# Reordering the work around the turning of chunk 1's keys and queries in an attention + MLP kernel on one core

## The chip, the cores and the metric

The kernel runs on one core of a Trainium2 chip. The metric is the device time of one execution in microseconds (us). Before the change four executions took 233.51, 233.23, 233.58 and 234.99 us; their median is 233.55 us. One further execution was recorded by the hardware profiler. It took 234.79 us, and 233.0 us of that are the span from the first to the last instruction of the program.

## The reference

Attention over 4 batches, 8 heads, 768 positions, 64 elements per head, followed by a two-layer MLP over all 3072 tokens:

```python
scores = scale * np.matmul(q, k.transpose(0, 1, 3, 2))
stream_keep = causal & (is_sink | in_win)           # first 4 keys, or the last 64
mask = np.where(retr[0, :, 0, 0, None, None], full_mask, stream_mask)
scores = np.where(mask[None, :, :, :], scores, -1000000000.0)
a = np.exp(scores - max); a = a / (a.sum + 1e-09)
attn = np.matmul(a, v)
x = attn.transpose(0, 2, 1, 3).reshape(B * S, H * D)   # 3072 x 512
h = x @ w_in                                        # 512 x 2048
g = np.maximum(0.01 * h, h)
out = g @ w_out                                     # 2048 x 512
```

Heads 0, 2 and 6 see all earlier keys; the other five see the first 4 keys (the sinks) and a window of 64. All inputs and the output are float32 in memory; the kernel computes in bfloat16 with float32 sums.

## The kernel before, in words

The 3072 tokens are cut into 8 chunks of 384 (half a batch each; the order is batch 0 first half, batch 1 first half, batch 0 second half, batch 1 second half, and then the same for batches 2 and 3). A chunk goes through attention, then "product 1" (x times w_in, 16 column tiles of 128, each closed by a leaky ReLU on ScalarE), then "product 2" (g times w_out, closed by a copy on VectorE and a store). The order of all instructions is written out by hand: each engine executes its own instructions in program order, and a semaphore wait holds up everything behind it on that engine. So "moving" a step means moving all its instructions on TensorE, VectorE and ScalarE alike.

Tiles that TensorE writes are PSUM banks with four tags, two banks each: `ph`, `psS`, `po`, `py`. A third user of a tag waits until the first has been emptied.

The start of the program treats chunk 0 in three tiles of 128 queries (objects `F0`, `F1`, `F2`), because its data arrive piecewise. `Fj.x_t` turns the finished attention rows of tile j (4 transposes on TensorE into a `py` bank, one copy by VectorE, "v", or ScalarE, "a"). `in_tile(q4, j)` is product 1 for tile j and column quarter q4 of w_in: 16 matmuls of 128x128 (L576) into one `ph` bank and one ScalarE instruction (L579). `in_tile(0, *)` needs the first quarter of w_in, `in_tile(1, *)` the second.

For chunk 1, `turn_pair(1, p, ...)` turns the keys or queries of the head pair p: three transposes (L203), one for each of three 128-row tiles that come by DMA. Keys are emptied in two halves (L190 on VectorE, L194 on ScalarE: "vv" both by VectorE, "aa" both by ScalarE); queries in one copy (L188 on VectorE, L192 on ScalarE) into `qt`. `zero_small(1)` clears two tiles of batch 1 on VectorE (L171, L172); `ats[2:]` are three tiles whose middle parts have to be zero (L736); `m_win0` is a mask; `sink_keys(1)` gathers the four sink keys of each head (L262, L266), `sink_values(1)` their values (L128). `a1` is the list of attention slots of chunk 1: a slot of a retrieval head computes scores into a `psS` bank (L329), ScalarE takes their exponential (L334), and VectorE multiplies by a causal mask (L337, L339). The value products follow six slots later.

All loads that convert float32 to bfloat16 are issued by POOL in program order at the head of the kernel (L638 to L655): chunk 0's tiles, the first quarter of w_in, chunk 1's k (three issues at L113), chunk 1's q (three at L113), the second quarter of w_in (L135), chunk 1's v, the rest of the weights, and then k, q and v of chunk 2.

Of the kernel before, what the change touches and what calls it, by code (L numbers as in the profile page):

```python
# [21 lines left out]
def kernel(  # L22
# [12 lines left out]
    nc = tc.nc  # L35
    B, H, S, D = q.shape
# [22 lines left out]
    def bank(tag, shape, dtype):  # L59
        return ps.tile(shape, dtype, name=tag, tag=tag, bufs=BANKS[tag])  # L60

    def bf(name, *shape):
        return one.tile([128, *shape], BF16, name=name)
# [13 lines left out]
    m_one = bf("m_one", 64)  # L77
    m_win = bf("m_win", 6, 64)
    m_win0 = bf("m_win0", 6, 64)
    m_sink = bf("m_sink", H)  # L80
    shift = bf("shift", 2, 128)
    kt = [[bf(f"kt{i}_{hh}", 4, S) for hh in range(2)] for i in range(2)]
    va = [bf(f"va{i}", 6, H, D + 1) for i in range(B)]
    vb = [bf(f"vb{i}", 5, H, D + 1) for i in range(B)]
    vs = [bf(f"vs{i}", H, D + 1) for i in range(2)]
    ksink = [bf(f"ksink{i}", 4 * SK) for i in range(2)]
    ats = [bf(f"ats{i}", 3, 4, 64) for i in range(5)]
# [38 lines left out]
    def sink_values(b, eng):  # L126
        n = H - 1
        eng.tensor_tensor(  # L128
            vs[b % 2][0:32, 1:H, 0:D],
            vsf[b].rearrange("p (o d) -> p o d", o=1).to_broadcast([32, n, D]),  # L130
            m_sink[0:32, 1:H].rearrange("p (h o) -> p h o", o=1).to_broadcast([32, n, D]),
            op=ALU.mult)
# [37 lines left out]
    def zero_small(i, eng):  # L170
        eng.memset(ksink[i][:], 0.0)  # L171
        eng.memset(vs[i][:], 0.0)  # L172
# [12 lines left out]
    def move(eng, dst, src, hh=None):  # L185

        if eng == "v" and hh is None:
            nc.vector.tensor_copy(dst, src)  # L188
        elif eng == "v":
            nc.vector.tensor_scalar_mul(dst, src, half[:, hh : hh + 1])  # L190
        elif hh is None:
            nc.scalar.activation(out=dst, in_=src, func=ACTF.Copy)  # L192
        else:
            nc.scalar.activation(out=dst, in_=src, func=ACTF.Copy, scale=half[:, hh : hh + 1])  # L194

    def turn_pair(n, p, tags, engs, nms="kq"):
        b, c = ORDER[n]
        if n not in qx:
            qx[n] = rot.tile([128, 4, CH], BF16, name="qt", tag="qt", bufs=1)
        for nm, tag, eng in zip(nms, tags, engs):  # L200
            pt = bank(tag, [128, 4, 128], BF16)
            for g in range(3):
                nc.tensor.transpose(pt[:, g, :], raw[nm, n][:, g, 2 * p : 2 * p + 2, :], ident[:])  # L203
            if nm == "k":
                for hh in range(2):
                    move(eng[hh], kt[b % 2][hh][:, p, CH * c : CH * c + CH].rearrange("p (g t) -> p g t", g=3), pt[:, 0:3, :], hh)
            else:
                move(eng, qx[n][:, p, :].rearrange("p (g t) -> p g t", g=3), pt[:, 0:3, :])
# [38 lines left out]
    def into(slots, extra):  # L247
        r, extra = [], list(extra)
        for j, s in enumerate(slots):
            r.append(s)  # L250
            if 5 * j >= 2 * len(slots) and extra:
                r.append(extra.pop(0))
                if len(extra) > len(slots) - j - 2:
                    r.append(extra.pop(0))
        return r + extra
# [14 lines left out]
    def sink_keys(b):  # L270
        for f in sink_keys_by(b):
            f()
# [282 lines left out]
    py = {}  # L555

    def in_slots(n, tags=("ph",)):
        def tick(t):
            if n not in gs:
                gs[n] = rot.tile([128, NG, CH], BF16, name="g", tag="g", bufs=2)  # L560
            ph = bank(tags[t % len(tags)], [128, 512], FP32)
            for g in range(KG):
                nc.tensor.matmul(ph[:, 0:CH], lhsT=w_in_bf[:, g, 128 * t : 128 * t + 128],  # L563
                                 rhs=xts[n][:, g, :] if n else xts[0][:, :, g, :], start=(g == 0), stop=(g == KG - 1))
            nc.scalar.activation(out=gs[n][:, t, :], in_=ph[:, 0:CH], func=ACTF.Prelu, alpha=0.01)  # L565

        return [lambda t=t: tick(t) for t in range(NG)]

    def in_tile(q4, j, tag="ph"):
        if 0 not in gs:  # L570
            gs[0] = rot.tile([128, NG, CH], BF16, name="g", tag="g", bufs=2)
        ph = bank(tag, [128, 4, 128], FP32)
        for x in range(4):
            t = 4 * q4 + x
            for g in range(KG):
                nc.tensor.matmul(ph[:, x, :], lhsT=w_in_bf[:, g, 128 * t : 128 * t + 128],  # L576
                                 rhs=xts[0][:, j, g, :], start=(x == 0 and g == 0),
                                 stop=(g == KG - 1), skip_group_check=True)
        nc.scalar.activation(out=gs[0][:, 4 * q4 : 4 * q4 + 4, 128 * j : 128 * j + 128], in_=ph[:],  # L579
                             func=ACTF.Prelu, alpha=0.01)  # L580
# [29 lines left out]
    def run(*lists):  # L610
        for l in lists:
            for f in l:
                f()

    def tail(ms, a):

        return [a[0], ms[0], a[1], ms[1], a[2], ms[2], ms[3], *a[3:]]

    def both(s, e):
        return lambda: (s(), e and e())  # L620
# [66 lines left out]
    F0, F1, F2 = (First(j) for j in range(3))  # L687
# [43 lines left out]
    F2.finish(0)  # L731
    F2.av(1)
    F2.finish(1)
    zero_small(1, nc.vector)
    for a in ats[2:]:
        nc.vector.memset(a[:, :, 1:3, :], 0.0)  # L736
    F1.x_t("py", "a")
    in_tile(0, 0)
    turn_pair(1, 0, ("psS",), ("vv",), "k")
    turn_pair(1, 1, ("psS",), ("aa",), "k")  # L740
    in_tile(0, 1)
    F2.x_t("py", "v")
    turn_pair(1, 2, ("psS",), ("vv",), "k")
    turn_pair(1, 3, ("py",), ("aa",), "k")
    in_tile(0, 2)
    turn_pair(1, 0, ("psS",), "v", "q")
    turn_pair(1, 1, ("py",), "v", "q")
    turn_pair(1, 3, ("psS",), "v", "q")
    turn_pair(1, 2, ("py",), "v", "q")
    nc.vector.tensor_copy(m_win0[:, 2:], m_one.rearrange("p (o t) -> p o t", o=1).to_broadcast([128, 4, 64]))  # L750
    sink_keys(1)
    sink_values(1, nc.vector)
    nc.vector.tensor_copy(vs[1][0:32, :, D], m_sink[0:32, :])
    p0 = in_slots(0)
    a1 = Attention(1, po_tags=("po", "po", "po", "py"), xt_eng="v").slots([0, 2, 6, 1, 3, 4, 5, 7], lag=6)


    run(a1[0:3])
    in_tile(1, 0)
    run(a1[3:5])  # L760
    in_tile(1, 1)
    run(a1[5:6])
    in_tile(1, 2)
# [28 lines left out]
    for n in range(2, NCH):  # L792
        a, extra = [], ()
# [10 lines left out]
        if n + 1 < NCH:  # L804
            a = Attention(n + 1, xt_eng="v", xt_tag="py", cross=n > 2).slots(lag=2 if n > 2 else 3)
            a = into(a, extra) if n > 2 else a
        ms = merge(in_slots(n), outs)
        keep = []
        if n == 2:
            a = [both(s, e) for s, e in zip(a, [None] * 16 + extra + [None] * 3)]  # L810
            ms, a, keep = ms[:-6], a[:-6], tail(ms[-6:-2], a[-6:]) + ms[-2:]
# [42 lines left out]
```

## Time and profile before

| quantity | value |
|---|---|
| median of four executions | 233.55 us (233.23 to 234.99) |
| the profiled execution, its own time | 234.79 us |
| its span | 233.0 us |
| TensorE (PE) busy | 223.6 us, 96% of the span |
| VectorE (DVE) busy | 98.8 us, 42% |
| ScalarE (ACT) busy | 127.5 us, 55% |
| GpSimd (POOL) busy | 71.1 us, 31% |
| granted TensorE clock | 0.999 of full speed |

A row of the timeline begins with the start in us from the span's start and the length in us; then come the engine, the line of the kernel, the operation, and output<-inputs. `x16` says how many instructions were merged. What stands in brackets is how long the engine idled before the row, and what ended that. `PEld` is the weight load that precedes a matmul. A row of the DMA list tells from which queue a transfer was issued, how often, the size of one, and the time from issue to landing. In the chain of waits each row is a piece of the path that ended last.

### The profile page before, as it was taken

The numbers are of one execution on the slowest core, as the hardware profiler recorded it, in microseconds if no ns is written. First come the engines' busy times: TensorE is split into PE (matmuls) and PEld (weight loads), VectorE is DVE, ScalarE is ACT, GpSimd is POOL, SyncE is SP. The second block draws the span as 40 slices with busy tenths as digits, with TensorE's granted clock in tenths as the row PEclk, the third lists the DMA queues.
The fourth block names the chain that finished last, engine by engine and source line by source line (L and its number), as shares of the span: only waits on it lengthen the run. The fifth ranks groups of instructions, "written<-read, shape, count | busy, mean of one in ns | idle before, by whom it ended". The sixth has DMA issues, their size and how long they took to land.

```text
span 233.0 us, 5091 instructions
## 1 busy us (share of the span) xinstructions
PE 223.6 (96%) x2054; PEld 139.3 (60%) x2080; DVE 98.8 (42%) x282; ACT 127.5 (55%) x275; POOL 71.1 (31%) x87
## 2 busy tenths in 40 slices
PE   6888999999999999999999999999999999999995
PEld 4666876644665676665556655666556665555554
DVE  7895568014566358358324451155212341111122
ACT  5766765722774886655355544765556763434300
POOL 8968534217319219439104800000000000000000
PEclk9999999999999999999999999999999999999999
DMA  9999999999999999999999992920210220111112
GB/s 130 151 165 178 203 207 169 180 130 160 150 149 257 180 160 131 173 177 158 135 142 188 172 172 57 209 65 17 68 59 0 65 80 20 45 45 45 45 47 91
DMA packets 109480, 28.98 MB, mean 124 GB/s; under 512 B 101248, under 2 KB 105744, under 8 KB 109456
## 3 DMA queue, kind: packets, MB, share of 16 engines
q0 software_dynamic: 77088, 13.39, 76.8%
q1 hardware_dynamic: 31312, 15.00, 32.5%
q10 hardware_dynamic: 1056, 0.26, 0.5%
q8 instruction: 16, 0.26, 0.5%
q14 instruction: 8, 0.07, 0.1%
HBM read 27.30 MB, written 6.29 MB: 144 GB/s over the span
## 4 chain that ended last, share of the span: by engine, by line
PE 86%; POOL 5%; DMA 4%; issue 1%; DVE 1%; ACT 0%; POOLq 0%
PE py L589 31%; PE ph L563 31%; PE po L298 7%; PE psS L329 5%; DMA w_in_bf<-in_moe_w_in_dram 4%; PE psS L589 3%; PE psS L364 3%; PE psS L563 2%; PE psS L309 2%; PE ph L576 1%; POOL kb L113 1%; POOL va L118 1%; POOL qb L113 1%; POOL k L104 1%; POOL q L105 1%
## 5 line engine op out<-in xcount | busy, mean ns | idle before, releaser
L563 PE MATMUL ph<-xt,w_in_bf 128*128 128x384 bf16 x448 | 90.4, 326 | 0.1
L589 PE MATMUL py<-w_out_bf,g 128*128 128x512 bf16 (+1 forms) x327 | 85.7, 374 | 1.2
L565 ACT ACTIVATE g<-ph 128x384 bf16<-128x384 f32 x112 | 55.0, 491 | 56.8 <-PE ph L563 56.4
L563 PEld LDWEIGHTS <-w_in_bf 128*128 128x128 bf16 x480 | 44.0, 98 | 30.7
L589 PEld LDWEIGHTS <-g 128*128 128x128 bf16 x416 | 35.8, 98 | 25.9
L334 ACT ACTIVATE at<-psS 128x384 bf16<-128x384 f32 x78 | 37.0, 488 | 17.4 <-PE psS L329 16.9
L595 DVE COPY o<-py 128x512 f32<-128x512 f32 (+1 forms) x22 | 14.9, 678 | 52.1 <-PE py L589 51.8
L113 POOL DMA_DIRECT2D kb<-in_k_dram x21 | 18.7, 908 | 32.2 <-DMA kd<-kb 31.6
L329 PE MATMUL psS<-qd,kt 128*128 128x384 bf16 (+2 forms) x90 | 23.2, 294 | 0.0
L118 POOL DMA_DIRECT2D va<-in_v_dram x24 | 21.4, 916 | 5.0 <-DMA w_out_bf<-in_moe_w_out_dram 1.8
L113 POOL DMA_DIRECT2D qb<-in_q_dram x21 | 18.6, 916 | 5.7 <-DMA w_in_bf<-in_moe_w_in_dram 1.8
L298 PE MATMUL po<-va,at 128*128 128x65 bf16 x228 | 19.3, 193 | 0.0
L369 ACT ACTIVATE ats<-psS 128x384 bf16<-128x384 f32 x35 | 16.9, 490 | 3.2 <-PE psS L364 2.9
L298 PEld LDWEIGHTS <-at 128*128 128x128 bf16 x234 | 14.9, 98 | 5.2 <-issue 0.2
L373 DVE TENSOR_TENSOR ats<-ats,m_win 128x384 bf16<-128x384 bf16 x35 | 12.4, 357 | 12.0 <-ACT ats L369 11.2
L237 DVE COPY kt<-kd 64x512 bf16<-64x512 bf16 x36 | 14.9, 413 | 2.0 <-DMA kd<-kb 1.4
L397 DVE TENSOR_TENSOR xs<-po,linv 128x384 bf16<-128x384 f32 x27 | 15.0, 557 | 0.9
L329 PEld LDWEIGHTS <-kt 128*128 128x128 bf16 x99 | 9.4, 98 | 7.4 <-issue 0.6
L364 PEld LDWEIGHTS <-kt 128*128 128x128 bf16 x210 | 10.5, 98 | 5.1 <-issue 0.2
L339 DVE TENSOR_TENSOR at<-at,m_caus 128x128 bf16<-128x128 bf16 x21 | 4.7, 224 | 20.1 <-ACT at L334 19.9
L298 PEld LDWEIGHTS <-ats 128*128 128x128 bf16 x210 | 10.5, 97 | 4.0 <-DVE xs L397 0.4
L337 DVE TENSOR_TENSOR at<-at,m_caus 128x256 bf16<-128x256 bf16 x21 | 6.1, 291 | 14.7 <-ACT at L334 14.7
(145 smaller groups left out, 204.3 us busy)
## 6 DMA issues: line engine op xcount, KB each, us to landing
out_dram<-o SPq DMA_DIRECT2D x23, 256.0 KB, 2.3
va<-in_v_dram POOLq DMA_DIRECT2D x24, 128.0 KB, 7.7
kb<-in_k_dram POOLq DMA_DIRECT2D x21, 128.0 KB, 5.5
qb<-in_q_dram POOLq DMA_DIRECT2D x21, 128.0 KB, 6.7
w_in_bf<-in_moe_w_in_dram POOLq DMA_DIRECT2D x4, 512.0 KB, 9.6
w_out_bf<-in_moe_w_out_dram POOLq DMA_DIRECT2D x4, 512.0 KB, 13.3
vb<-va SPq DMA_DIRECT2D x8, 195.0 KB, 4.0
vb<-va SPq DMA_DIRECT2D x4, 130.0 KB, 3.2
```

The lines of the kernel that those rows point to most:

```text
L113: nc.gpsimd.dma_start(out=t[:, g], in_=nat[nm][b, c, :, :, g])
L118: nc.gpsimd.dma_start(out=va[b][:, 3 * c + g, :, 0:D], in_=nat["v"][b, c, :, :, g])
L237: nc.vector.tensor_copy(kt[b % 2][hh][r, :, o : o + 128], raw["kx", n][r, g])
L298: nc.tensor.matmul(o, lhsT=lhsT, rhs=rhs, start=first, stop=False, skip_group_check=True)
L329: nc.tensor.matmul(s[:, off : off + w], lhsT=kt[i][hh][:, p, 128 * kj : 128 * kj + 128], rhs=q_of(n, p, lo, CH), start=(j == 0), stop=(j = ...
L334: nc.scalar.activation(out=a[:, 0:off], in_=s[:, 0:off], func=ACTF.Exp, scale=SM)
L364: nc.tensor.matmul(s[:, 64 * m : 64 * m + 64], lhsT=kt[i][hh][:, p, k0 : k0 + 128], rhs=q_of(n, p, 64 * m, 64 * m + 64), start=(m == 0), s ...
L369: nc.scalar.activation(out=av_, in_=s[:, 0:CH].rearrange("p (j e f) -> p j e f", j=3, e=2), func=ACTF.Exp, scale=SM)
L397: nc.vector.tensor_tensor(xs[:], po[:, :, :, 0:D], linv.to_broadcast([128, 3, 2, D]), op=ALU.mult)
L563: nc.tensor.matmul(ph[:, 0:CH], lhsT=w_in_bf[:, g, 128 * t : 128 * t + 128], rhs=xts[n][:, g, :] if n else xts[0][:, :, g, :], start=(g == ...
L565: nc.scalar.activation(out=gs[n][:, t, :], in_=ph[:, 0:CH], func=ACTF.Prelu, alpha=0.01)
L589: nc.tensor.matmul(py[n][:, 0 : c1 - c0], lhsT=gs[n][:, ng, 128 * tt : 128 * tt + 128], rhs=w_out_bf[:, ng, c0:c1], start=(ng == 0), stop= ...
```

## The change

The set of steps stays the same; their order between the end of chunk 0's attention and the second quarter of product 1 changes. Four things differ.

- The third x (`F2.x_t`) and `in_tile(0, 1)` go in front of the first turning of chunk 1's keys.
- The four turnings of q directly follow those of k. They use the two `py` banks alone (before: `psS` and `py` in turns), and the second is emptied by ScalarE instead of VectorE. All four key pairs use `psS`; of the fourth pair one half is emptied by VectorE, where ScalarE did both.
- `zero_small(1)` stands between the turnings of k and those of q instead of ahead of them.
- The clearing of `ats[2:]` and the filling of `m_win0` follow the first three slots of `a1`; `sink_values(1)` and the column beside it follow the next two.

```diff
     F2.finish(1)
+    F1.x_t("py", "a")
+    in_tile(0, 0)
+    F2.x_t("py", "v")
+    in_tile(0, 1)
+    turn_pair(1, 0, ("psS",), ("vv",), "k")
+    turn_pair(1, 1, ("psS",), ("aa",), "k")
+    in_tile(0, 2)
+    turn_pair(1, 2, ("psS",), ("vv",), "k")
+    turn_pair(1, 3, ("psS",), ("va",), "k")
     zero_small(1, nc.vector)
+    turn_pair(1, 0, ("py",), "v", "q")
+    turn_pair(1, 1, ("py",), "a", "q")
+    turn_pair(1, 3, ("py",), "v", "q")
+    turn_pair(1, 2, ("py",), "v", "q")
+    sink_keys(1)
+    p0 = in_slots(0)
+    a1 = Attention(1, ...).slots([0, 2, 6, 1, 3, 4, 5, 7], lag=6)
+    run(a1[0:3])
     for a in ats[2:]:
         nc.vector.memset(a[:, :, 1:3, :], 0.0)
-    F1.x_t("py", "a")
-    in_tile(0, 0)
-    turn_pair(1, 0, ("psS",), ("vv",), "k")
-    turn_pair(1, 1, ("psS",), ("aa",), "k")
-    in_tile(0, 1)
-    F2.x_t("py", "v")
-    turn_pair(1, 2, ("psS",), ("vv",), "k")
-    turn_pair(1, 3, ("py",), ("aa",), "k")
-    in_tile(0, 2)
-    turn_pair(1, 0, ("psS",), "v", "q")
-    turn_pair(1, 1, ("py",), "v", "q")
-    turn_pair(1, 3, ("psS",), "v", "q")
-    turn_pair(1, 2, ("py",), "v", "q")
     nc.vector.tensor_copy(m_win0[:, 2:], ...)
-    sink_keys(1)
+    in_tile(1, 0)
+    run(a1[3:5])
     sink_values(1, nc.vector)
     nc.vector.tensor_copy(vs[1][0:32, :, D], m_sink[0:32, :])
-    p0 = in_slots(0)
-    a1 = Attention(1, ...).slots([0, 2, 6, 1, 3, 4, 5, 7], lag=6)
-    run(a1[0:3])
-    in_tile(1, 0)
-    run(a1[3:5])
     in_tile(1, 1)
     run(a1[5:6])
     in_tile(1, 2)
```

No DMA is added, removed or moved: the instructions of POOL and of the store queue (SP) are the same ones in the same order. From `in_tile(1, 0)` on TensorE's instructions are the same in the same order.

More of the change, by code (lines that the diff above doesn't have):

```diff
@@ L733 @@
     F2.finish(1)
-    zero_small(1, nc.vector)
-    for a in ats[2:]:
-        nc.vector.memset(a[:, :, 1:3, :], 0.0)
     F1.x_t("py", "a")
     in_tile(0, 0)
+    F2.x_t("py", "v")
+    in_tile(0, 1)
     turn_pair(1, 0, ("psS",), ("vv",), "k")
     turn_pair(1, 1, ("psS",), ("aa",), "k")
-    in_tile(0, 1)
-    F2.x_t("py", "v")
+    in_tile(0, 2)
     turn_pair(1, 2, ("psS",), ("vv",), "k")
-    turn_pair(1, 3, ("py",), ("aa",), "k")
-    in_tile(0, 2)
-    turn_pair(1, 0, ("psS",), "v", "q")
-    turn_pair(1, 1, ("py",), "v", "q")
-    turn_pair(1, 3, ("psS",), "v", "q")
+    turn_pair(1, 3, ("psS",), ("va",), "k")
+    zero_small(1, nc.vector)
+    turn_pair(1, 0, ("py",), "v", "q")
+    turn_pair(1, 1, ("py",), "a", "q")
+    turn_pair(1, 3, ("py",), "v", "q")
     turn_pair(1, 2, ("py",), "v", "q")
-    nc.vector.tensor_copy(m_win0[:, 2:], m_one.rearrange("p (o t) -> p o t", o=1).to_broadcast([128, 4, 64]))
     sink_keys(1)
-    sink_values(1, nc.vector)
-    nc.vector.tensor_copy(vs[1][0:32, :, D], m_sink[0:32, :])
     p0 = in_slots(0)
@@ L758 @@
     run(a1[0:3])
+    for a in ats[2:]:
+        nc.vector.memset(a[:, :, 1:3, :], 0.0)
+    nc.vector.tensor_copy(m_win0[:, 2:], m_one.rearrange("p (o t) -> p o t", o=1).to_broadcast([128, 4, 64]))
     in_tile(1, 0)
     run(a1[3:5])
+    sink_values(1, nc.vector)
+    nc.vector.tensor_copy(vs[1][0:32, :, D], m_sink[0:32, :])
     in_tile(1, 1)
```

## The prediction

> **What bounds the kernel now.** I read the busy shares first (PE 96%), then the chain of waits around the changed place, then the timeline of PE, DVE and ACT there. The chain:
>
> ```profile
> 13.50 10.40 DMA w_in_bf<-in_moe_w_in_dram
> 23.90 0.05 issue
> 23.95 1.07 PE ph L576 x16
> ```
>
> The end hangs on a transfer: the second quarter of w_in, issued at 13.50, lands at 23.90, and in_tile(1,0) starts at 23.95. Behind it PE runs nearly without a hole. By busy time in windows, PE has 6.00 of 6.00 us in 24 to 30 and again in 30 to 36, and 11.95 of 12.00 in 36 to 48. Comparing starts, I find in 24 to 55 three small holes: 0.06 at 28.97 (two av rows end, the next starts at 29.03), 0.16 at 32.91, 0.22 at 36.24, together 0.44 us.
>
> The changed work lies in front of 23.95:
>
> ```profile
> 15.64 1.07 PE L576 MATMUL ph<-xt,w_in_bf 128*128 128x128 bf16 x16 [0.20 <-DVE linv L542]
> 17.90 0.44 PE L203 MATMUL psS<-ident,kb 128*128 128x128 bf16 x2 [1.20 <-DMA kb<-in_k_dram]
> 18.84 0.40 PE L203 MATMUL psS<-ident,kb 128*128 128x128 bf16 x4 [0.50 <-DMA kb<-in_k_dram]
> 19.07 1.06 PE L576 MATMUL ph<-xt,w_in_bf 128*128 128x128 bf16 x16
> 19.97 0.39 PE L550 MATMUL py<-ident,xs 128*128 128x128 bf16 x4
> ...
> 20.87 1.05 PE L576 MATMUL ph<-xt,w_in_bf 128*128 128x128 bf16 x16
> 21.76 0.33 PE L203 MATMUL psS<-ident,qb 128*128 128x128 bf16 x3
> ...
> 22.54 0.32 PE L329 MATMUL psS<-qt,kt 128*128 128x384 bf16 x1
> 23.07 0.70 PE L329 MATMUL psS<-qt,kt 128*128 128x256 bf16 x3 [0.20 <-DVE qt L188]
> ```
>
> The reader sees k's tiles awaited twice (1.20 and 0.50 us), then work without a hole up to the first score at 22.54. The third score starts at 23.44 (a narrower window gives this start) and streams 0.16, so PE would be free at 23.60. The weight load of in_tile(1,0) waits 0.67 us for the transfer:
>
> ```profile
> 23.95 0.90 PEld L576 LDWEIGHTS <-w_in_bf 128*128 128x128 bf16 x16 [0.67 <-DMA w_in_bf<-in_moe_w_in_dram]
> ```
>
> That is 0.35 us of slack (23.95 less 23.60). Making the front shorter can only enlarge it.
>
> **The change, part by part.**
>
> *Third x and in_tile(0,1) into the wait for k.* Sixteen matmuls from 19.07 to 19.97, 0.90 us, and four transposes, 0.22 (4 x 0.055), in all 1.12 us. in_tile(0,0) ends at 16.53 (15.64 + 0.89); F2's xs are ready at 16.05 (15.63 + 0.42 on DVE); so x_t runs 16.53 to 16.75 and in_tile(0,1) to 17.64, before k's first tile at 17.90. The filling works: 1.12 us leave the stretch behind 19.07. By itself this is a gain of 1.12 us in front of 23.95, and 0 behind it, because the transfer covers it. Without that cover it would be worth what the next wait leaves of it, computed now.
>
> *q straight behind k.* k pairs 0 and 1 turn at 18.84 to 19.07 as before; in_tile(0,2) then runs 19.07 to 19.96; pair 2 to 20.13. Pair 3 needs the bank that ACT empties by 20.33 (19.75 + 0.57 = 20.32) and turns at 20.4. Issues of q start at 10.91, 11.77 and 12.64 and land 8.8, 8.8 and 8.7 us later (the DMA list in narrow windows), so the third tile is there at 21.34. q's turning can thus start at most 0.42 us earlier than at 21.76. But its emptying has something in front of it. DVE, in the old order:
>
> ```profile
> 16.06 0.28 DVE L171 MEMSET ksink<- 128x272 uint32 x1
> 16.40 0.49 DVE L172 MEMSET vs<- 128x520 bf16 x1
> 16.88 0.63 DVE L736 MEMSET ats<- 128x192 uint32 x3
> 19.11 0.74 DVE L190 TENSOR_SCALAR kt<-psS,half 128x384 bf16<-128x384 bf16 x2 [1.60 <-PE psS L203]
> ...
> 20.75 0.74 DVE L190 TENSOR_SCALAR kt<-psS,half 128x384 bf16<-128x384 bf16 x2
> 22.13 0.36 DVE L188 COPY qt<-psS 128x384 bf16<-128x384 bf16 x1 [0.64 <-PE psS L203]
> 22.40 0.35 DVE L188 COPY qt<-py 128x384 bf16<-128x384 bf16 x1
> ```
>
> The two memsets lay under the wait for k, free. Now they lie behind k and ahead of q. From transposes to the first emptying took 0.37 (20.38 to 20.75), so pair 2 starts on DVE at 20.34. Three L190 (two of pair 2, one of pair 3, 0.33 apart and 0.41 long) end at 21.41; the memsets take 0.34 to the next start and 0.49, end 22.24. q's pair 0 is then emptied 22.24 to 22.60 (before from 22.13). Pair 3 needs its `py` bank, pair 2 follows: PE starts at 22.65 (0.05 from DVE's end to PE, as 22.49 to 22.54) and takes two times three transposes, 0.33. First score 22.98, against 22.54. ACT's exponential followed the score by 0.36 (22.54 to 22.90), and the third score that by 0.54 (22.90 to 23.44, the bank): 22.98 + 0.36 + 0.54 = 23.88, plus 0.16 of streaming, 24.04. in_tile(1,0) starts at 24.04 against 23.95: **+0.09 us**. What is late next is a1's exponentials, by 0.44; the fifth score needs the third's bank, emptied at about 24.7, and PE reaches it at 25.1.
>
> *One emptying of q on ACT, one half of k on DVE.* ACT loses one L194 (0.57) and gets a copy of 128x384 that the trace does not show on it. From below L334's 0.48, from above the 0.60 of L579; I take 0.57, L194's, the same shape from the same type. It starts at 21.8 and ends by 22.4, before PE needs the bank at 22.8. At either end it costs 0; if it had no cover, 0.2.
>
> *Fills behind the scores.* Three memsets (0.22 each) and the mask (0.21) come after the third mask on DVE, at about 24.9 to 25.7; the next L337 ran at 26.06. The zeros are used by value products from 31.78, m_win0 by L373 at 29.01. sink_values (0.61) and the column (0.17) follow L339 at 26.45 and end by 27.4; the L337 behind them ran at 27.32 and its result is used after 28.9. All 0, hidden by those waits; without that cover at most 0.1.
>
> *Queues.* POOL and SP keep their instructions. POOL's issues that wait for PE are chunk 2's k (25.50, after k is turned, by 20.8) and q (29.50, after q is turned, 23.0). Both have over 4 us: 0.
>
> *The sum.* +0.09 from the late scores, 0 from the rest. Bounds: if the weight quarter lands earlier in unprofiled executions, the two fronts are compared bare, 24.04 less 23.60, +0.44. From below, -0.05 (the step from landing to start) and -0.44 if all holes behind closed, -0.49. I take +0.1: the nearest row is the transfer's. The profiled execution would go from 234.79 to 234.9; that one is 1.24 us above the median. On the median: **233.65 us**.
>
> [...] PE does only transposes from 19.96 to 22.98, 3.0 us. In the old trace that stretch was 16.53 to 19.07, 2.5 us, and the granted clock was 1.00 in 16.71 to 20.12 (PE busy 1.72 of 3.41 us). [...]
>
> **The rivals.** A change of 0.5% is 1.17 us, about what a measurement here tells from none.
>
> *The front decides in every execution* (the quarter lands earlier without the profiler): +0.44, 234.0. For it: the median lies 1.24 us below the profiled time, and something was faster there. Against: k and q come through the same queue, and would come earlier too.
>
> *The clock falls* in the emptier stretch before 23.95. Price: the twenty dummy matmuls at the start.
>
> ```profile
> 1.06 3.66 PE L151 MATMUL psS<-blank 128*128 128x256 bf16 x20 [1.06 <-DVE blank L632]
> 27.14 0.60 PE L309 MATMUL psS<-qt,ksink 128*128 128x256 bf16 x4
> ```
>
> Cold, 19 steps of a 256-wide matmul took 3.39 us (3.66 less the last one's 0.27), 0.178 each; later 0.11 each ((0.60 - 0.27)/3). One such stretch behind 23.95 costs 19 x 0.068 = 1.3 us: 234.95, **slower**. It decides once the transposes-only stretch is longer than what the old trace survived (2.5 us); I expect 3.0. Against it: the transposes, twelve of q and six of k, are spread over the stretch, as the six of k were in the old one.
>
> *The filled wait is worth its length.* in_tile(1,0) at 22.83 and the holes closed: 233.55 - 1.12 - 0.44 = 232.0, **faster**. For it: 1.7 us of waits for k. Against it: the 10.40 us transfer, issued before anything that changes, and the memsets.
>
> *The change doesn't do what it says*, q being emptied no earlier, is part of my forecast.
>
> **How the numbers follow.** Forecast 0.70, front decides 0.12 (both within 0.5%), clock 0.11, full worth 0.07. Faster 0.07, same 0.82, slower 0.11. The range holds the first two with their bounds, -0.49 and +0.44 on 233.55, widened at either end by the 0.35 by which the three closest of the four runs differ: 232.7 to 234.4.
>
> **What would show it.** In the new profile: x_t and in_tile(0,1) between 16.5 and 17.7; DVE's memsets at 21.4 to 22.3 with the first q copy behind them; the first score near 23.0 and the third near 23.9; the quarter landing at 23.9 and in_tile(1,0) within 0.2 us of 24.0; PE full behind. I am wrong if the quarter lands at another time, if the clock is below 1.00 behind 24, or if a new hole opens between 24 and 36.

## The result, and the profile after

Over 54 executions the changed kernel has a median of 234.88 us (233.35 to 238.55). Over 78 executions of the kernel before, the first four among them, it is 233.88 us (232.91 to 236.97). The ratio is 1.0028 with a 95% interval of 1.0015 to 1.0040: slower, by less than 0.5%. Ratios, here and below, leave out executions over 1.5% above the fastest of their kernel (eight of the 54, two of the 78); the medians leave out none, and differ by 1.0 us. The median lies outside the range of the prediction (232.7 to 234.4).

The profiled execution shows nothing of this. It took 234.04 us (that of before 234.79), and its span is 0.8 us shorter.

The chain of waits of the changed kernel around the change (start, length, what):

```profile
10.05 7.87 DMA kb<-in_k_dram
17.97 0.40 PE psS L203 x4
18.37 0.89 PE ph L576 x16
19.26 0.18 PE psS L203 x3
19.47 1.08 DVE kt L190 x3
20.57 0.58 ACT kt L194
21.15 0.39 ACT qt L192
21.58 0.49 PE py L203 x6
22.08 0.18 PE psS L329
22.27 0.50 ACT at L334
22.82 0.32 PE psS L329
23.14 0.99 PE ph L576 x16
```

This chain no longer comes from the weight quarter. It runs from the last tile of k through the emptying of k on DVE, then ScalarE's half and its copy of q, the last turnings and the third score. But the two paths are nearly tied: the third score has streamed at 22.98, the quarter lands at 23.02, and the weight load of in_tile(1,0) still waits for the quarter:

```profile
23.06 0.90 PEld L576 LDWEIGHTS <-w_in_bf 128*128 128x128 bf16 x16 [0.77 <-DMA w_in_bf<-in_moe_w_in_dram]
```

The slack that the kernel before had here (0.35 us) is gone. TensorE's timeline of the same kernel:

```profile
15.60 1.06 PE L576 MATMUL ph<-xt,w_in_bf 128*128 128x128 bf16 x16
16.50 0.39 PE L550 MATMUL py<-ident,xs 128*128 128x128 bf16 x4
16.72 1.06 PE L576 MATMUL ph<-xt,w_in_bf 128*128 128x128 bf16 x16
17.61 0.76 PE L203 MATMUL psS<-ident,kb 128*128 128x128 bf16 x6
18.20 1.06 PE L576 MATMUL ph<-xt,w_in_bf 128*128 128x128 bf16 x16
19.10 0.74 PE L203 MATMUL psS<-ident,kb 128*128 128x128 bf16 x6
19.67 0.28 PE L203 MATMUL py<-ident,qb 128*128 128x128 bf16 x2
20.53 0.40 PE L203 MATMUL py<-ident,qb 128*128 128x128 bf16 x4 [0.58 <-DMA qb<-in_q_dram]
21.58 0.49 PE L203 MATMUL py<-ident,qb 128*128 128x128 bf16 x6 [0.65 <-ACT qt L192]
21.91 0.49 PE L329 MATMUL psS<-qt,kt 128*128 128x384 bf16 x3
22.82 0.32 PE L329 MATMUL psS<-qt,kt 128*128 128x384 bf16 x1 [0.41 <-ACT at L334]
```

The third x and in_tile(0,1) fill the wait for k, as announced. But the waits are not gone: from 19.10 to 22.98 TensorE has eighteen transposes and four score matmuls, with three waits among them (0.58, 0.65, 0.41). The weight quarter lands at 23.02 here and in_tile(1,0) starts at 23.06; before, the two were 23.90 and 23.95. The shorter span is this earlier landing and no merit of the change: from the start of in_tile(1,0) to the end the spans have 209.06 us before (233.01 - 23.95) and 209.18 after (232.24 - 23.06).

What the profile hides stands in the granted clock of the single executions of the changed kernel:

| mean granted clock | executions of 54 | median |
|---|---|---|
| 0.998 to 1.000 | 32 | 234.06 us |
| 0.992 or 0.993 | 16 | 235.87 us |
| 0.986 | 6 | 237.68 us |

The steps are about 1.8 us, and 0.007 of a span of 233 us is 1.6 us of missing clock, by estimate 3.3 us at a clock of 0.50, the one that the low stretches of e10, e13 and e17 show below. The overall median lies between the first two rows because only 32 of 54 executions run at full clock. Those 32 alone have a median inside the predicted range. (The clocks of the 78 executions before are not known.)

### The profile page after: what moved, and what is told of

Read it like the earlier page. It is cut to its first block, busy times and chain, and to the rows that moved or that the text cites. A ratio compares the mean times of both kernels' runs of the same rounds, so it can differ in the third digit from the quotient of the medians.

```text
span 232.2 us, 5092 instructions
## 1 busy us (share of the span) xinstructions
PE 223.9 (96%) x2054; PEld 139.8 (60%) x2080; DVE 98.4 (42%) x282; ACT 127.5 (55%) x275; POOL 71.2 (31%) x87
## 4 chain that ended last, share of the span: by engine, by line
PE 88%; POOL 4%; DMA 3%; DVE 1%; issue 1%; ACT 1%; POOLq 0%
PE py L589 31%; PE ph L563 31%; PE po L298 7%; PE psS L329 6%; DMA kb<-in_k_dram 3%; PE psS L589 3%; PE psS L364 3%; PE psS L563 2%; PE psS L309 2%; PE ph L576 2%; POOL va L118 1%; POOL k L104 1%; POOL q L105 1%; POOL kb L113 1%; DVE xs L397 0%
## 5 line engine op out<-in xcount | busy, mean ns | idle before, releaser
L237 DVE COPY kt<-kd 64x512 bf16<-64x512 bf16 x36 | 13.7, 380 | 0.6
```

## The experiments

All are edits of one of the two kernels. "Low clock" means an execution with a mean granted clock below 0.997. Full-clock medians are compared with the full-clock executions of the kernel before on the same chip.

**e1: the kernel before, again.**

> The kernel before, unchanged, to see the granted clock of its single executions. Clock theory (in the changed kernel about 4 of 10 executions run one window of some 3.4 us, or two, at half clock, and the kernel before nearly never does): granted clock 0.999 or 1.000 in at least 9 of 10 executions, ratio 1.000. Late-scores theory (the clears ahead of q's emptying put the first scores 0.4 us later in every execution): says nothing on the clock, ratio 1.000.

Measured: ratio 1.0001 (0.9982 to 1.0021), no low clock in 12 executions, nor in the 35 others of the kernel before in that session. Over all sessions of the experiments it was 3 of 124, all three in the session of e13 to e16 (3 of 35 there). Low clock is rare before the change.

**e2: dummies in the waits.**

```diff
     zero_small(1, nc.vector)
+    idle("ph", 6)
     turn_pair(1, 0, ("py",), "v", "q")
     turn_pair(1, 1, ("py",), "a", "q")
+    idle("ph", 6)
     ...
-    run(a1[0:3])
+    run(a1[0:2])
+    idle("ph", 4)
+    run(a1[2:3])
```

> The changed kernel with 16 dummy matmuls (6 ahead of q's first turning, 6 between the second and the third, 4 ahead of the third score), about 1.7 us of array work put into waits. Clock theory: no execution below 0.999, median back to 233.4 to 234.1, ratio 0.998 to 1.002. Late-scores theory: the dummies do nothing about DVE, ratio 1.002 to 1.005, and if anything slower.

Measured: no low clock in 12 executions; ratio 1.0027 (1.0001 to 1.0053); full-clock median 234.18, against 233.59. With work for TensorE that computes nothing, no execution of the 12 lost the clock (22 of 54 of the changed kernel did). The time is not repaired: a second, smaller loss remains at full clock.

**e3: q turned by plain matmuls.**

```diff
-            pt = bank(tag, [128, 4, 128], BF16)
+            pt = bank(tag, [128, 4, 128], BF16 if nm == "k" else FP32)
...
+                    nc.tensor.matmul(pt[:, g, :], lhsT=raw[nm, n][:, g, 2 * p : 2 * p + 2, :], rhs=ident[:],
+                                     start=(g == 0), stop=(g == 2), skip_group_check=True)
```

> The changed kernel with q turned by twelve plain matmuls against the identity (float32 banks) in place of twelve transposes; the same places, the same 128 columns each. Clock theory in the form that transposes do not count as activity: the share of executions below 0.999 falls from 4 in 10 to under 1 in 10, ratio near 1.001. Clock theory in the form that only idle time counts: the share stays at 3 to 5 in 10, ratio near 1.003. Late-scores theory: ratio 1.003 to 1.005, since emptying float32 banks is no faster.

Measured: 5 of 12 at low clock, ratio 1.0037 (1.0014 to 1.0060). So the low clock does not hang on the turnings being transposes.

**e4: the clears back under the wait for k.**

```diff
     in_tile(0, 0)
+    zero_small(1, nc.vector)
     F2.x_t("py", "v")
...
-    zero_small(1, nc.vector)
     turn_pair(1, 0, ("py",), "v", "q")
```

> The changed kernel with the two clears (ksink, vs) on DVE back under the wait for k, ahead of the third x. Late-scores theory: q's first pair is emptied 0.3 to 0.6 us earlier, third score the same, ratio back to 1.000 and no slow executions. Clock theory: TensorE's stretch of transposes alone hardly shortens (0.4 us of about 2.8), the share below 0.999 stays between 2 and 5 in 10, ratio 1.001 to 1.004.

Measured: 1 of 12 at low clock, ratio 1.0030 (1.0005 to 1.0055), full-clock median 234.12 against 233.59. So the late-scores theory as it was put, with the clears as the cause, failed: it wanted 1.000 here. The profile shows why: the third score starts 4.93 us after the landing of k's last tile (22.15 against 17.22), where the profile after has 4.89. Undoing the clears alone does not bring the scores earlier. (In this profile in_tile(1,0) then waits 0.81 us for the weight quarter, but the quarter came 6.0 us behind k, where 5.1 is usual.)

**e5 and e16: the changed kernel, again, on two further chips.**

> The changed kernel, unchanged, beside the kernel before on one chip. Clock theory: 3 to 6 of some 12 executions with a granted clock of 0.993 or 0.986, these 1.5 to 4 us longer; the others at 1.000 within 0.5 us of the kernel before; if the profiled execution is a slow one, TensorE's clock in it stands at half for about 3.4 us close behind 20 us. Late-scores theory: all executions at full clock, 0.4 us longer than before.

> The changed kernel on the chip of the three others. Clock theory: 3 to 6 of 12 below 0.999, those 1.5 us or more above the rest; the rest 0.1 to 0.5 us above the kernel before. Late-scores theory: all at full clock and 0.4 us above.

Measured: 3 of 7 and 3 of 12 at low clock. Ratios 1.0067 (1.0040 to 1.0094) and 1.0013 (0.9983 to 1.0043). The full-clock medians are 234.79 (of four) against 233.83, and 234.48 against 233.94.

**e6: the first part alone** (kernel before, with the third x and in_tile(0,1) moved ahead of k).

```diff
     in_tile(0, 0)
+    F2.x_t("py", "v")
+    in_tile(0, 1)
     turn_pair(1, 0, ("psS",), ("vv",), "k")
     turn_pair(1, 1, ("psS",), ("aa",), "k")
-    in_tile(0, 1)
-    F2.x_t("py", "v")
```

> The kernel before with the first part of the change alone (third x and product 1 of the second tile ahead of k's turning; in_tile(0,2), the turnings of q, the clears and the fills as before). Clock theory: in_tile(0,2) still stands between the turnings of k and q, so no stretch of 3.4 us is as empty as in the changed kernel: under 2 of 12 executions below 0.999, ratio 0.999 to 1.001. Late-scores theory: no clear stands ahead of q, ratio 1.000. A theory that the filled wait for k is itself to blame (k, when it lands early, waits for TensorE): ratio 1.002 to 1.004 at full clock.

Measured: 0 of 12, ratio 1.0002 (0.9989 to 1.0016). Filling the wait for k gains nothing and costs nothing.

**e7: dummy transposes in place of dummy matmuls**, at the places of e2.

```diff
+    def turns(tag, n):
+        s = bank(tag, [128, 4, 128], BF16)
+        for _ in range(n):
+            nc.tensor.transpose(s[:, 0, :], blank[:, 0:128], ident[:])
...
+    turns("ph", 12)    # and 12, 8
```

> The changed kernel with 32 dummy transposes (12, 12 and 8, the array time of the dummy matmuls of the earlier fill) in the same three places. If transposes do not count as activity: 3 to 6 of 12 executions below 0.999, median 234.5 to 235.5. If they count: none below 0.999, median 233.6 to 234.3.

Measured: 0 of 12, ratio 1.0019 (0.9995 to 1.0043). With the transposes no execution was at low clock, as with the matmuls (0 of 12 each). In its profile in_tile(1,0) starts 0.69 us after the landing, so here the dummies are in the way of the third score.

**e8: clears early, six dummies ahead of q, six behind the third score.**

```diff
+    idle("ph", 6)
     turn_pair(1, 0, ("py",), "v", "q")
...
     run(a1[0:3])
+    idle("ph", 6)
```

> The changed kernel with the two clears back under the wait for k, 6 dummy matmuls ahead of q's first turning and 6 behind the third score, in the wait for the weight quarter. Clock theory: none below 0.999. With both causes gone (no low clock, scores not late) the ratio is 0.998 to 1.001; if a third cause is left in the full-clock executions, 1.002 to 1.003.

Measured: 0 of 6, but ratio 1.0067 (1.0049 to 1.0085). In its profile in_tile(1,0) starts 0.44 us after the landing (22.98 against 22.54), so the dummies themselves are in the way. The experiment says that the clock holds, and nothing on a third cause.

**e9: the first part, and in_tile(0,2) between the turnings of k.**

```diff
     turn_pair(1, 1, ("psS",), ("aa",), "k")
+    in_tile(0, 2)
     turn_pair(1, 2, ("psS",), ("vv",), "k")
     turn_pair(1, 3, ("py",), ("aa",), "k")
-    in_tile(0, 2)
```

> The first part of the change (third x and product 1 of the second tile ahead of k) plus one move: in_tile(0,2) between the second and third turning of k, as in the changed kernel, instead of behind the fourth. Clears, fills, banks and q's emptying as before. Clock theory: this one move is what empties the stretch between 19 and 23 us, so 2 to 6 of 12 executions fall below 0.999 (with the tile behind the fourth turning it was 0 of 12), ratio 1.002 to 1.005. Late-scores theory: nothing stands ahead of q on DVE, ratio 1.000, none below 0.999.

Measured: 1 of 12, ratio 1.0002 (0.9974 to 1.0030). The move that I held to be the cause does not do it alone, as far as twelve executions tell. e13, e14 and e15 add one more part each to this kernel.

**e13: e9 and the clears between k and q.**

```diff
-    zero_small(1, nc.vector)
     for a in ats[2:]:
...
+    zero_small(1, nc.vector)
     turn_pair(1, 0, ("psS",), "v", "q")
```

> Base: first part of the change plus in_tile(0,2) between the turnings of k (1 of 12 below 0.999, ratio 1.0002). Added: the two clears between the turnings of k and of q. Clock theory with the clears as what stretches the empty time: q's emptying 0.8 us later, 3 to 6 of 12 below 0.999, ratio 1.002 to 1.005. Late-scores theory: full-clock median 0.3 to 0.5 us above the kernel before. If neither, ratio 1.000.

Measured: 4 of 12 at low clock, ratio 1.0012 (0.9978 to 1.0045), full-clock median 234.15 against 233.94. In its profiled execution the weight quarter landed unusually late (24.36, 6.8 us behind k, where 5.1 is usual), which alone made a long wait on TensorE; so the low clock of this one execution is no measure of the clears. Its third score starts 4.31 us after k's last tile, as early as in e9 (4.29): with four banks for q the clears do not make the scores late.

**e14: e9 and the emptying of the changed kernel.**

```diff
-    turn_pair(1, 3, ("py",), ("aa",), "k")
-    turn_pair(1, 0, ("psS",), "v", "q")
-    turn_pair(1, 1, ("py",), "v", "q")
-    turn_pair(1, 3, ("psS",), "v", "q")
+    turn_pair(1, 3, ("psS",), ("va",), "k")
+    turn_pair(1, 0, ("py",), "v", "q")
+    turn_pair(1, 1, ("py",), "a", "q")
+    turn_pair(1, 3, ("py",), "v", "q")
```

> Same base; added: q turned through the two py banks with the second pair emptied by ScalarE, and the fourth k pair emptied half by VectorE, half by ScalarE. Clock theory with the banks as cause: PE waits twice more, 2 to 5 of 12 below 0.999. Late-scores theory with the banks as cause: full-clock median 0.2 to 0.4 us above the kernel before. If the clears alone matter: ratio 0.999 to 1.001 and at most 1 of 12.

Measured: 4 of 12, ratio 1.0030 (0.9999 to 1.0061), full-clock median 234.47 against 233.94. In its profile in_tile(1,0) starts 0.22 us after the landing (23.32 against 23.10), at the moment when the third score has streamed. The third score starts 5.13 us after k's last tile, against 4.29 in e9: the two banks with the split emptying make the scores late and thin out the stretch (TensorE is busy for 0.94 of the 2.00 us in 20 to 22, in e9 for 1.44).

**e15: e9 and the fills behind the scores.**

```diff
     run(a1[0:3])
+    for a in ats[2:]:
+        nc.vector.memset(a[:, :, 1:3, :], 0.0)
+    nc.vector.tensor_copy(m_win0[:, 2:], ...)
     in_tile(1, 0)
     run(a1[3:5])
+    sink_values(1, nc.vector)
```

> Same base; added: the zero fills, the mask and the sink values behind the first scores. Clock theory and late-scores theory both: nothing (TensorE waits for none of them), ratio 0.999 to 1.001, at most 1 of 12 below 0.999. A full-clock median 0.3 us or more above the kernel before would make the fills the third cause.

Measured: 2 of 12, ratio 1.0000 (0.9969 to 1.0032), full-clock median 234.04 against 233.94. The fills cost nothing that this run can tell (its interval is 0.3% to either side), and 2 of 12 is not apart from the 3 of 35 of the kernel before in that session.

**e10: the suspected cause doubled and more.** The pair of clears ahead of q's emptying is done three times.

```diff
     zero_small(1, nc.vector)
+    zero_small(1, nc.vector)
+    zero_small(1, nc.vector)
     turn_pair(1, 0, ("py",), "v", "q")
```

> The changed kernel with the pair of clears ahead of q's emptying done three times, 1.6 us more on DVE. Both theories: the scores come 1.6 us later and every execution 1.5 to 1.7 us. [...] Late-scores theory alone: median 235.2 to 235.8 at full clock.

Measured: low clock in 4 of 4 executions (granted clock 0.993 in two, 0.985 and 0.986 in the others), median 236.77, ratio 1.0121 (1.0079 to 1.0162). In the changed kernel it was 22 of 54; with the stretch emptier still it was all of them.

**e11, e12, e17, e18: four more profiled executions of the changed kernel.**

> The changed kernel, one more profiled execution. Clock theory: with a chance of 0.4 TensorE's clock stands at half for 3.4 us (or twice that) somewhere between 20 and 31 us; matmuls of 128x384 take twice as long there and the span is 1.5 us longer per window. Late-scores theory: full clock, in_tile(1,0) decided by the third score and not by the weight quarter.

> The same as the look before it, a second draw: chance of 0.4 for a window at half clock between 20 and 31 us by the clock theory; full clock by the late-scores theory.

> Third look at the changed kernel. Clock theory: with a chance of 0.4 half clock for 3.4 or 6.8 us, beginning between 22 and 24 us, the sixteen matmuls of in_tile(1,0) then taking 1.9 instead of 1.06 us, span 233.5 to 236. Late-scores theory: full clock.

> Fourth look at the changed kernel, the same expectations as for the third.

Measured: 234.27, 233.98, 234.95 and 235.90 us. The first two ran at full clock and show what the profile after shows. e17 caught the low clock. TensorE's timeline of e17:

```profile
21.39 0.49 PE L329 MATMUL psS<-qt,kt 128*128 128x384 bf16 x3
22.30 0.35 PE L329 MATMUL psS<-qt,kt 128*128 128x384 bf16 x1 [0.41 <-ACT at L334]
22.51 1.89 PE L576 MATMUL ph<-xt,w_in_bf 128*128 128x128 bf16 x16
24.19 0.85 PE L329 MATMUL psS<-qt,kt 128*128 128x256 bf16 x3
24.83 1.56 PE L576 MATMUL ph<-xt,w_in_bf 128*128 128x128 bf16 x16
26.23 0.33 PE L329 MATMUL psS<-qt,kt 128*128 128x256 bf16 x2
26.39 1.06 PE L576 MATMUL ph<-xt,w_in_bf 128*128 128x128 bf16 x16
```

The same sixteen matmuls take 1.89 us in in_tile(1,0) and 1.06 two tiles later. Busy time in stretches of e17 (start and end, length, busy us of PE with its instructions, of PEld, DVE, ACT and POOL, then the granted clock, the DMA share and GB/s), read in narrow steps for the edges of the low clock:

```profile
22.40:22.50 0.10, 0.10 (x1) 0.00 (x0) 0.10 (x2) 0.10 (x1) 0.00 (x0) 0.80 2.62 156
22.50:22.60 0.10, 0.10 (x3) 0.10 (x3) 0.08 (x1) 0.10 (x1) 0.00 (x0) 0.50 2.60 152
...
25.80:25.90 0.10, 0.10 (x4) 0.10 (x3) 0.07 (x1) 0.00 (x0) 0.10 (x1) 0.63 1.16 195
25.90:26.00 0.10, 0.10 (x4) 0.10 (x3) 0.10 (x2) 0.00 (x0) 0.10 (x1) 1.00 1.39 225
```

A tenth of a microsecond with clock 0.80 is 0.6 at full and 0.4 at half: the clock falls at 22.46. By the same reckoning it is back at 25.87 (0.63 is 0.74 at half): an estimated 3.41 us at half clock (22.40 to 25.90 has 0.51 in the mean). The stretch of that length just before the fall:

```profile
19.05:22.46 3.41, 1.82 (x19) 1.17 (x18) 2.91 (x11) 2.19 (x6) 2.00 (x3) 1.00 1.79 182
```

TensorE was busy for 1.82 of 3.41 us, 53%. The dummies, and leaving in_tile(0,2) where it was, raise that in about the same place. In turn the same 3.40 us of e2, of e7 and of e6 (part one alone), each from its own kernel:

```profile
19.00:22.40 3.40, 3.40 (x38) 2.74 (x38) 2.90 (x11) 2.18 (x5) 1.67 (x3) 1.00 1.77 182
```

```profile
19.00:22.40 3.40, 3.17 (x54) 2.93 (x51) 2.71 (x9) 2.18 (x5) 1.62 (x4) 1.00 1.76 184
```

```profile
19.00:22.40 3.40, 2.71 (x38) 2.23 (x37) 2.08 (x8) 2.48 (x6) 2.56 (x4) 1.00 1.75 181
```

100%, 93% and 80%, and no low clock in 36 executions of the three. (The traces of e2 and e8 hold no records of the clock; such a trace shows 1.00 in any case, so the 1.00 in e2's row says nothing by itself. The trace of e7 has records.)

In e13 the clock fell as well, at 23.59, and in e10 at 21.71. The stretches just before and behind the fall, e13 first:

```profile
20.17:23.59 3.42, 1.72 (x14) 0.91 (x14) 3.02 (x13) 1.86 (x5) 1.03 (x2) 1.00 2.04 172
23.59:27.00 3.41, 2.60 (x22) 2.37 (x23) 0.00 (x0) 0.67 (x2) 1.96 (x3) 0.50 1.36 203
```

```profile
18.30:21.71 3.41, 1.73 (x23) 1.20 (x21) 2.79 (x9) 2.20 (x5) 2.42 (x4) 1.00 1.56 195
21.71:25.12 3.41, 2.10 (x14) 1.54 (x14) 2.49 (x9) 1.34 (x3) 1.21 (x2) 0.50 1.97 177
```

Ahead of the fall TensorE was busy for 50% and 51% of the stretch. Read in narrow steps as in e17, the clock is back at 30.41 in e13 (0.93 in 30.40 to 30.50) and at 28.54 in e10 (0.82 in 28.50 to 28.60): an estimated 6.8 us at half clock in each, twice as long as in e17. The price in e17: from the start of in_tile(1,0) to the end 210.64 us (233.15 - 22.51), against 209.0 to 209.6 in the six other profiled executions of the changed kernel; some 1.0 to 1.6 us for its 3.41 us at half clock.

A stretch as empty was not enough by itself. This one is from the profile after, which kept the clock (1.00 in it, and again 1.00 in 22.40 to 25.90):

```profile
19.64:23.05 3.41, 1.76 (x19) 1.05 (x17) 2.91 (x11) 2.04 (x5) 1.96 (x3) 1.00 1.88 178
```

TensorE was busy for 52% of it. What sets the executions that lose the clock apart from those that keep it was not shown.

e18 shows what spreads the executions at full clock. Its TensorE timeline:

```profile
19.47 0.61 PE L203 MATMUL psS<-ident,kb 128*128 128x128 bf16 x5 [1.18 <-DMA kb<-in_k_dram]
...
24.69 1.00 PE L576 MATMUL ph<-xt,w_in_bf 128*128 128x128 bf16 x15
```

k's last tile landed 1.7 us later than in the profile after (19.63 against 17.93). The whole front moved with it, and the span is 234.1 us at a clock of 1.000. From in_tile(1,0) on it takes 209.43 us, as ever.

## Why the prediction was wrong, point by point

*What bounds the kernel*: right. In seven profiled executions of the changed kernel in_tile(1,0) starts 0.05 to 0.19 us after the weight quarter lands (0.08 in the mean; before 0.05), whether that is at 22.46 or at 24.61. The two conditions of the start are now nearly tied, though: the third score has streamed within 0.1 us of that start in each of the seven. All behind it takes as long as before (209.0 to 209.6 us in the six at full clock; 209.1 and 209.3 in two profiles before).

*The filled wait is worth nothing*: right, as e6 shows (1.0002, 0.9989 to 1.0016).

*q's first emptying behind the clears*: right in size. Counted from the landing of k's last tile (18.80 before, 17.93 after), the third score was forecast for 5.08 and came at 4.89; the first copy of q for 3.44, and came at 3.36. What I overlooked is that ScalarE's half of the fourth k pair waits for VectorE's half, 0.62 us, and that its copy of q comes behind it. This stands in ScalarE's timeline of the changed kernel:

```profile
20.57 0.58 ACT L194 ACTIVATE kt<-psS,half 128x384 bf16<-128x384 bf16 x1 [0.62 <-DVE kt L190]
21.05 0.48 ACT L192 ACTIVATE qt<-py 128x384 bf16<-128x384 bf16 x1
```

So "at either end it costs 0" was wrong for the split emptying: TensorE's last two turnings wait 0.65 us for that copy, and e14 loses time by these edits alone (1.0030, with an interval that just reaches 1). VectorE's copy behind the clears ended only 0.05 us later (21.58 against 21.53), so undoing one of the two gains little, as e4 showed.

*The fills behind the scores cost 0*: right (e15, 1.0000).

*The sum of +0.1*: the medians rose by 1.0 us, most of it by the clock (below). In the executions at full clock the changed kernel loses more than +0.1, too: +0.2 us against the kernel before in the first comparison (234.06 against 233.88, all executions), +0.5 in e16, +1.0 in the four of e5. In the profiled executions the landing and the start differ by only 0.03 us more than before, so most of this rest is not explained by them. The kernels part by how long after k's last tile the third score starts in their profiles:

| kernels | third score after k's last tile | full-clock median against before |
|---|---|---|
| before, e6, e9, e13, e15 | 4.3 to 4.6 us | 0.0 to +0.2 us |
| changed, e2, e3, e4, e14 | 4.9 to 5.1 us | +0.2 to +1.0 us |

(e7, e8 and e10 are not in it, because what they add is itself in the way.)

The weight quarter lands 5.1 us behind k's last tile in most profiles, and the score streams for 0.16: the second group has no slack left. Whenever the quarter comes somewhat sooner behind k than that, in_tile(1,0) starts late in these kernels alone. That is the rival that the front decides (+0.44), and it is near in size. But no run shows when the quarter lands without the profiler, and the medians are of 4 to 32 executions with landings that spread by 2 us. It stays open.

*The clock* is the step that failed. The sum put it at nothing; that 3.0 us with transposes alone keep the clock was shown by no run, and the runs showed low clock in 22 of the first 54 executions. As a rival the prediction put it as one thing that happens to the kernel or does not, with a chance of 0.11. It is a thing that happens to a share of the executions: 29 of 77 of the changed kernel (22 of 54, 3 of 7, 3 of 12, 1 of the 4 further profiles), 3 of 124 of the kernel before, at some 1.8 us where the granted clock is 0.992 or 0.993 and 3.6 where it is 0.986. With that share the median must move by itself, and the clock of 1.00 in the old trace was one draw. The stretch that the prediction took as survived, 16.71 to 20.12 with TensorE busy for 1.72 of 3.41 us, was half busy (50%), about as those ahead of the three falls (50 to 53%). That this trace kept its clock there proved nothing on other executions, nor on stretches longer than 2.5 us. (k came late in it; in e1's profile no 3.41 us around there are under 69% busy.)

The forecast length of the stretch with transposes alone was good (3.0 us; 2.8 measured, 19.10 to 21.91). The point from which it decides was not: I set it by the length of the stretch without other matmuls, as one trace had it. In e17 TensorE was busy for 53% of the 3.41 us ahead of the fall, with no wait over 0.7 us in it. And it is not the transposes as such: with dummy transposes added no execution was at low clock (e7, 0 of 12), and with plain matmuls in place of q's transposes 5 of 12 were (e3).

Why the share is as large as 29 of 77 was not shown.

The price was put low as well. I had 1.3 us from the dummies at the start of the kernel, of which the last ones already ran faster (each takes 421 ns in 2.0 to 3.4 us of that trace, and 272 or 273 in the last five). With TensorE busy throughout, as in e17, 3.41 us at half clock lose an estimated 1.7 us of matmul time, and the steps between the medians are 1.8 us; but e17's own loss, 1.0 to 1.6 us, does not exclude 1.3.

*No part was shown to do it alone*: with in_tile(0,2) between the turnings of k it was 1 of 12, with the clears or the emptying added 4 of 12 each, and with the clears undone in the changed kernel 1 of 12 again. Counts of twelve do not set 1 and 4 apart, and the two with 4 were taken where the kernel before had 3 of 35; so which part weighs most is not shown. No version of these beat the kernel before; the nearest are e6, e9 and e15, at 1.000.

## What to carry to other kernels

Before work is moved out of a stretch in order to fill a wait elsewhere, look at how busy TensorE stays in the stretch that it leaves: here the clock fell three times behind 3.4 us that were 50 to 53% busy, and two other traces kept it over 3.41 us with 50% and 52%. One profiled execution at full clock does not prove that a kernel keeps it; read the granted clock of many executions, and compare medians at full clock and the share below apart from each other. And a wait that a later transfer covers is worth nothing when it is filled, however long it looks.

## What the runs showed of the hardware that was not expected

- Half clock behind a stretch of 3.4 us in which TensorE was half busy: 53% in e17, 51% in e10 and 50% in e13. In e17 it had waits of 0.42, 0.67 and 0.41 us, and none longer. In the profile before 50% and in that after 52% of such a stretch were busy, and the clock stayed at 1.00.
- In the three profiles that caught it the clock stood at half for an estimated 3.41 us (e17) and for 6.8 us (e10, e13). Behind the fall TensorE was busy throughout in e17, and for 62% and 76% of the first 3.41 us in e10 and e13.
- The same transfer, issued at 13.50 us in the profile before and at 13.51 in that after, landed at 23.90 and at 23.02; in e13 it landed at 24.36. In the changed kernel at full clock the span moved with it: 232.2 us with the landing at 22.46 (e12), 234.1 us at 24.61 (e18).
